# A fused top-k attention and two gated layers: the normalising half of the softmax one block later, two elementwise steps moved to ScalarE

## The chip, the cores and the metric

The kernel runs on one core of one Trainium2 chip. The metric is the device time of one execution in microseconds; the number of a kernel is the median of its runs. Engines are called as in the profile: PE (matmul) and PEld (its weight loads), DVE (VectorE), ACT (ScalarE), POOL (GpSimd), SP (which issues the DMAs here).

## What is computed

The reference is attention that keeps the 32 largest scores of each row, followed by two dense layers on the result. The shapes are 4 batches, 8 heads, 576 positions and a head size of 64; all 2304 rows of 512 values go through the layers.

```python
def _attn_ref(q, k, v):                      # top_k = 32, scale = 1 / sqrt(64)
    scores = scale * np.matmul(q, k.transpose(0, 1, 3, 2))
    kth = np.partition(scores, -top_k, axis=-1)[..., -top_k:-top_k + 1]
    scores = np.where(scores >= kth, scores, -1000000000.0)
    scores = scores - np.max(scores, axis=-1, keepdims=True)
    attn = np.exp(scores)
    attn = attn / (np.sum(attn, axis=-1, keepdims=True) + 1e-09)
    return np.matmul(attn, v)

def _moe_ref(x, w_gate, w_val, w_out):       # 512 -> 1536 -> 512
    gate = 1.0 / (1.0 + np.exp(-(x @ w_gate)))
    return gate * (x @ w_val) @ w_out

def _moe2_ref(x, w_in, w_out):               # 512 -> 2048 -> 512
    r = np.maximum(x @ w_in, 0.0)
    return (r * r) @ w_out
```

## The kernel before

**Tiling.** The 2304 rows are 18 tiles of 128 rows. `CHUNKS` groups them into 11 chunks: chunks 0 to 3 hold one tile each, chunks 4 to 10 two tiles. Attention works on a unit of one tile and one head, a "block" of 128 rows by 576 scores; there are 144 blocks, 8 in each of chunks 0 to 3 and 16 in each of chunks 4 to 10. Once all blocks of a chunk are through, the chunk goes through both layers (`moe`), while the blocks of the following chunks run beside it.

**One block.** `scores` (L313) multiplies queries and keys into one PSUM tile `sp` (a single buffer, L331), and ACT copies it to the SBUF tile `S` (two buffers, L334). `softmax` (L337) then finds the 32nd largest value on DVE: four MAX8 (L344), each giving the next eight maxima, with three MATCH_REPLACE8 (L350) between them, which strike out what was found. From the first and last maximum POOL makes the two biases `bs` (L354). ACT turns the scores below the threshold into a huge number (Relu, L357), POOL subtracts that from the scores (L358; this is the last reader of `S`), ACT takes the exponential and its row sum (L359). That is the first half. In the second half DVE adds 1e-9 to the sum (L363, tile `rz`) and inverts it (L366), and POOL multiplies the block with it, in two pieces (L375, `we` for the last 64 columns and `W` for the first 512). For chunks 4 and on (`DMT = 4`) ACT then rounds the block to fp16 (L381), POOL takes the remainder (L382), and a DMA on SP's queue transposes both (L387); for the second head of a pair the 64 end columns get the same treatment (L397 to L399), and the last unit of a pair issues the loads of the values (`load_values`). The matmul with the values is `values` (L471).

**Order of the blocks.** The generator `attention` (L965) issues, for block n: `head(n + 1)` (key and query loads, query transposes, scores and the copy to `S` of the next block), then `tail` of blocks that lag by two (`TLAG = 2`; at the end of a pair of heads its `values`), then `softmax` of block n. `last_max` holds the last MAX8 issued, and the first MAX8 of the next block is placed behind it, without a semaphore, so that DVE works on one block at a time.

**The layers.** In the first layer `l1_pair` (L686 on) makes two 128-wide columns of gate and value in PSUM (`pg`, `pv`, L705); ACT takes tanh (L715), POOL turns it into the scaled sigmoid by one addition and one multiplication (L716), DVE multiplies it with the value (L717), ACT rounds to fp16 (L720) and POOL takes the remainder (L721). In the second layer `l2_pair` (L803) PE makes `ph` (L812), ACT takes Relu (L821) and its square rounded to fp16 (L823), POOL squares Relu in fp32 in place (L824) and takes the remainder (L825). The products of `l1_acc` (L745) and `l2_acc` (L833) use both parts. Chunk 0 has a function of its own, `moe32`, which the diff leaves alone. Each chunk has 6 pairs in the first layer and 8 in the second; a pair is 128 by 512 in chunks 4 to 10 and 128 by 256 in chunks 1 to 3.

**What sets the order on the engines.** The program hands its instructions to a planner, which orders each engine's queue by the priority of the instruction (in the order of issue, attention moved ahead by `attend` with `AHEAD = 1000`) and by the time at which its own model of the chip has the operands ready. Each queue is then fixed and runs in order.

Of the kernel before, what the change touches and what calls it, by code (L numbers as in the profile page):

```python
# [10 lines left out]
F32 = mybir.dt.float32  # L11
# [3 lines left out]
AF = mybir.ActivationFunctionType  # L15
ALU = mybir.AluOpType
AX = mybir.AxisListType
PSUM = bass.MemoryType.PSUM
NOSYNC = mybir.DependencyInfo(mybir.DependencyClass.NoSync, mybir.DependencyReason.DATA)
DRAM = bass.MemoryType.DRAM  # L20

P = 128
# [42 lines left out]
DMT = 4  # L65
# [5 lines left out]
TB = 15  # L71
# [3 lines left out]
def tile_topk_attention__then__two_moe_layers(  # L75
# [14 lines left out]
    nc = tc.nc  # L90
# [20 lines left out]
    apool = ctx.enter_context(tc.tile_pool(name="apool", bufs=2))  # L111
# [134 lines left out]
    class Pair:  # L246
# [90 lines left out]
        def softmax(self, j, i, ss):  # L337
# [4 lines left out]
            cur = ss  # L342
            for r in range(TOPK // 8):
                m8 = nc.vector.max(mx[:, r], cur)  # L344
                if r == 0 and last_max:
                    tc.add_manual_dep(
                        m8.ins, last_max[0].name, NOSYNC, reason="one row block at a time"
                    )
                if r < TOPK // 8 - 1:
                    nc.vector.match_replace(wk, mx[:, r], cur, NEG)  # L350
                    cur = wk
            last_max[:] = [m8.ins]
            bs = apool.tile([P, 4], F32, tag="bs", bufs=3, name=f"bs_{tt}_{h}")
            nc.gpsimd.tensor_tensor(  # L354
                bs[:, 0:2], mx.rearrange("p a b -> p (a b)")[:, 0 : TOPK : TOPK - 1], bsc, op=ALU.mult
            )
# [2 lines left out]
            nc.scalar.activation(  # L359
                wk, wk, AF.Exp, bias=bs[:, 0:1], scale=SCALE, accum_out=bs[:, 2:3]  # L360
            )
            rz = apool.tile([P, 1], F32, tag="rz", bufs=3, name=f"rz_{tt}_{h}")
            nc.vector.tensor_scalar(  # L363
                rz, bs[:, 2:3], 1e-9, 1.0 if self.ci < DMT else 1.0 / PSC, op0=ALU.add, op1=ALU.mult
            )
            nc.vector.reciprocal(rz, rz)  # L366
            if self.ci < DIAG:
                dg = apool.tile([P, P], F32, tag="we", bufs=WE, name=f"dg_{tt}_{h}")
                nc.gpsimd.tensor_scalar(dg, ident, rz, 1.0, op0=ALU.mult, op1=ALU.mult)
                return wk, dg  # L370
# [315 lines left out]
    def moe_head(ci, x):  # L686
        m = ahead[ci] = Moe()
        m.gp, m.queue = None, []
        tts = chunks[ci]
        N = len(tts) * P  # L690
        ig = scales["wg"][1]
        xs, ix = x
        gsc = mpool.tile([P, 1], F32, tag="gsc", bufs=2, name=f"gsc_{ci}")
        nc.vector.scalar_tensor_tensor(gsc, ix, 0.5, ig, op0=ALU.mult, op1=ALU.mult)

        def l1_pair(fp, gh=None):
            pg = ps_w.tile([P, 512], F32, tag="wk", name=f"pg_{ci}_{fp}")
            pv = ps_w.tile([P, 512], F32, tag="wk", name=f"pv_{ci}_{fp}")
            for pp, wd in ((pg, "wg"), (pv, "wv")):
                for e in range(2):  # L700
                    f0 = (2 * fp + e) * P
                    n = 0
                    for c in range(KM):
                        for a, b_ in SPLIT:
                            nc.tensor.matmul(  # L705
                                pp[:, e * N : (e + 1) * N],
                                wblk(wd, a, c, f0, P),
                                xs[:, b_, c, :],
                                start=(e == 0 and n == 0),
                                stop=(n == 3 * KM - 1),  # L710
                                skip_group_check=True,
                            )
                            n += 1
            th = mpool.tile([P, 2 * N], F32, tag="f32w", bufs=2, name=f"th_{ci}_{fp}")
            nc.scalar.activation(th, pg[:, 0 : 2 * N], AF.Tanh, scale=gsc)  # L715
            nc.gpsimd.tensor_scalar(th, th, 1.0, float(2.0 ** (-TB - 1)), op0=ALU.add, op1=ALU.mult)  # L716
            nc.vector.tensor_tensor(th, pv[:, 0 : 2 * N], th, op=ALU.mult)  # L717
            if gh is None:
                gh = mpool.tile([P, 2, 2 * N], F16, tag="hi", bufs=HIB, name=f"gh_{ci}_{fp}")
            nc.scalar.copy(gh[:, 0], th)  # L720
            nc.gpsimd.tensor_tensor(gh[:, 1], th, gh[:, 0], op=ALU.subtract)  # L721
            return gh

        m.N, m.ix, m.l1_pair = N, ix, l1_pair

    def moe(ci, nxt=None):
# [76 lines left out]
        def l2_pair(fp):  # L803
# [17 lines left out]
            nc.scalar.activation(r, ph[:, 0 : 2 * N], AF.Relu, scale=float(2.0 ** (7 - 2 * TB)))  # L821
            gh = mpool.tile([P, 2, 2 * N], F16, tag="hi", bufs=HIB, name=f"rh_{ci}_{fp}")
            nc.scalar.activation(gh[:, 0], r, AF.Square)  # L823
            nc.gpsimd.tensor_tensor(r, r, r, op=ALU.mult)  # L824
            nc.gpsimd.tensor_tensor(gh[:, 1], r, gh[:, 0], op=ALU.subtract)  # L825
            return gh

# [137 lines left out]
    def attention():  # L965
# [10 lines left out]
        ready = {}  # L976
        work = {}
        lagging = []

        def keys(pi):  # L980
            if pi < len(pairs):
# [63 lines left out]
        for n, (pr, pi, j, i) in enumerate(units):  # L1045
            with tc.high_priority(offset=int(up[0])):
                head(n + 1)
                while lagging and n - lagging[0] >= (TLAG if units[lagging[0]][0].ci >= DMT else 1):
                    tail(lagging.pop(0))
            work[n] = pr.softmax(j, i, ready.pop(n))  # L1050
            lagging.append(n)
            yield
        while lagging:
            tail(lagging.pop(0))
        yield
# [145 lines left out]
```

## Time and profile before

| | us |
|---|---|
| three runs | 1345.93, 1340.33, 1340.26 |
| their median | 1340.33 |
| the profiled execution, its own time | 1336.54 |
| the span of its trace | 1334.4 |
| busy: PE, DVE, POOL, ACT | 1180.9, 1045.8, 953.4, 791.8 |
| mean granted clock of TensorE, share of full speed | 0.938 |

The trace covers the span; 2.1 us of the profiled execution lie outside it. A share of busy time is a mean over stages with different limits: the first 300 us also prepare the weights, up to 1165 us attention and layers run side by side, and after that only the layers of the last two chunks are left. A wait is put down to the instruction that released it.

### The profile page before, as it was taken

What the parts mean: (1) busy time and instruction counts of PE and PEld (TensorE: products, weight loads), DVE (VectorE), ACT (ScalarE), POOL (GpSimd) and SP (SyncE); (2) the same over time, 40 slices, a digit from 0 to 9 for tenths busy, and PEclk for the clock granted to TensorE, in tenths of its full rate; (3) what the DMA queues carried; (4) which work ended last, traced back from release to release, by engine and by line L of the source; (5) the groups of instructions that cost most, each with busy time, mean ns of one, the idle gap of its engine ahead of it and who ended that gap; (6) DMA issues with size and microseconds to landing.
All of it is one profiled execution on the core that took longest, in us unless ns stands there. A gap on an engine that the chain in (4) does not pass through costs nothing. (4 is left out here: it accounts for less than half of the span.)

```text
span 1334.4 us, 28839 instructions
## 1 busy us (share of the span) xinstructions
PE 1180.9 (88%) x10525; PEld 939.5 (70%) x10525; DVE 1045.8 (78%) x2258; ACT 791.8 (59%) x1592; POOL 953.4 (71%) x1164
## 2 busy tenths in 40 slices
PE   6657878978979889899965999999999999999998
PEld 4535766767868858667853767776876787787775
DVE  6999999999898988978889887888898988601010
ACT  4875767777666666655645665665666666523122
POOL 1887877886678797778767795787879788824223
PEclk9755989989999999999985999999999999999999
DMA  6967871256566765596854667787465655330300
GB/s 187 347 248 246 269 208 43 76 185 229 175 194 148 172 167 108 123 219 155 200 111 109 150 157 162 152 209 159 101 165 128 115 126 141 74 126 1 142 1 16
DMA packets 260717, 201.66 MB, mean 151 GB/s; under 512 B 205536, under 2 KB 213728, under 8 KB 260576
## 3 DMA queue, kind: packets, MB, share of 16 engines
q1 hardware_dynamic: 260576, 199.82, 56.1%
q8 instruction: 83, 1.36, 0.4%
q14 instruction: 58, 0.48, 0.1%
HBM read 143.65 MB, written 23.07 MB: 125 GB/s over the span
## 5 line engine op out<-in xcount | busy, mean ns | idle before, releaser
L344 DVE MAX8 mx<-W 128x8 f32<-128x576 f32 x432 | 327.3, 758 | 8.2
L358 POOL TENSOR_TENSOR W<-S,W 128x576 f32<-128x576 f32 x144 | 206.9, 1437 | 42.2 <-ACT W L357 35.7
L812 PE MATMUL ph<-x,wi_w 128*128 128x256 f16 (+1 forms) x1920 | 206.7, 261 | 9.4 <-ACT x L784 7.3
L350 DVE MATCH_REPLACE8 W<-mx,W 128x576 f32<-128x576 f32 x288 | 213.7, 742 | 0.0
L833 PE MATMUL acc<-w2t,rh 128*128 128x512 f16 x816 | 196.4, 382 | 5.9 <-DMA w2t<-w2s 5.4
L812 PEld LDWEIGHTS <-wi_w 128*128 128x128 f16 x1920 | 168.1, 100 | 42.0 <-issue 11.6
L331 PE MATMUL sp<-kst,qt 128*128 128x288 f32 x608 | 130.0, 334 | 32.2 <-ACT S L334 27.9
L705 PE MATMUL pg<-xs,wg_w 128*128 128x256 f16 (+1 forms) x1440 | 156.4, 260 | 2.1 <-POOL xs L669 1.1
L705 PE MATMUL pv<-xs,wv_w 128*128 128x256 f16 (+1 forms) x1440 | 152.5, 257 | 1.6 <-ACT th L715 0.6
L359 ACT ACTIVATE W<-W,bs 128x576 f32<-128x576 f32 x144 | 111.5, 775 | 67.8 <-POOL W L358 67.2
L357 ACT ACTIVATE W<-S,bs 128x576 f32<-128x576 f32 x144 | 111.4, 774 | 56.2 <-POOL bs L354 55.6
L382 POOL TENSOR_TENSOR w<-W,w 128x512 f16<-128x512 f32 x112 | 131.0, 1170 | 17.1 <-ACT w L381 16.8
L745 PEld LDWEIGHTS <-wo_w 128*128 128x128 f16 x1440 | 124.6, 99 | 25.1 <-issue 12.0
L705 PEld LDWEIGHTS <-wg_w 128*128 128x128 f16 x1440 | 124.5, 99 | 20.5 <-issue 2.2
L705 PEld LDWEIGHTS <-wv_w 128*128 128x128 f16 x1440 | 122.8, 98 | 20.4 <-issue 5.7
L833 PEld LDWEIGHTS <-rh 128*128 128x128 f16 x816 | 77.9, 98 | 83.5 <-issue 4.1
L745 PE MATMUL acc<-gh,wo_w 128*128 128x256 f16 (+1 forms) x1200 | 123.5, 257 | 10.1 <-POOL gh L721 8.2
L331 PEld LDWEIGHTS sp<-kst,qt 128*128 128x128 f32 x608 | 93.3, 200 | 44.6 <-ACT S L334 31.0
L344 DVE MAX8 mx<-S 128x8 f32<-128x576 f32 x144 | 107.4, 746 | 13.6 <-ACT S L334 13.5
L824 POOL TENSOR_TENSOR r<-r 128x512 f32<-128x512 f32 (+1 forms) x80 | 73.4, 919 | 57.4 <-ACT rh L823 57.2
L717 DVE TENSOR_TENSOR th<-pv,th 128x512 f32<-128x512 f32 (+1 forms) x60 | 36.2, 603 | 98.7 <-PE pv L705 96.0
L350 DVE MATCH_REPLACE8 W<-mx,S 128x576 f32<-128x576 f32 x144 | 106.9, 743 | 0.3 <-issue 0.3
(325 smaller groups left out, 2202.9 us busy)
## 6 DMA issues: line engine op xcount, KB each, us to landing
w2t<-w2s SPq DMA_DIRECT2D x80, 512.0 KB, 5.0
kst<-ks SPq DMA_DIRECT2D x104, 288.0 KB, 3.1
v<-vs SPq DMA_DIRECT2D x40, 288.0 KB, 3.3
qn<-in_q_dram SPq DMA_DIRECT2D x128, 64.0 KB, 2.6
wi_r<-in_moe_w_in_dram SPq DMA_DIRECT2D x16, 512.0 KB, 6.9
w_r<-in_moe_w_out_dram SPq DMA_DIRECT2D x16, 512.0 KB, 4.4
wg_r<-in_moe_w_gate_dram SPq DMA_DIRECT2D x12, 512.0 KB, 7.8
wv_r<-in_moe_w_val_dram SPq DMA_DIRECT2D x12, 512.0 KB, 6.7
```

The costliest lines, as they stand in the source:

```text
L331: nc.tensor.matmul(sp[:, e, 0:HALF], l, r, start=(x == 0), stop=(x == len(ops) - 1))
L344: m8 = nc.vector.max(mx[:, r], cur)
L350: nc.vector.match_replace(wk, mx[:, r], cur, NEG)
L357: nc.scalar.activation(wk, ss, AF.Relu, bias=bs[:, 1:2], scale=-BIG)
L358: nc.gpsimd.tensor_tensor(wk, ss, wk, op=ALU.subtract)
L359: nc.scalar.activation(wk, wk, AF.Exp, bias=bs[:, 0:1], scale=SCALE, accum_out=bs[:, 2:3])
L382: nc.gpsimd.tensor_tensor(w16[:, 1], wk[:, 0:SM], w16[:, 0], op=ALU.subtract)
L705: nc.tensor.matmul(pp[:, e * N : (e + 1) * N], wblk(wd, a, c, f0, P), xs[:, b_, c, :], start=(e == 0 and n == 0), stop=(n == 3 * KM - 1), ...
L745: nc.tensor.matmul(acc[:, d // 2, (d % 2) * N : (d % 2 + 1) * N], wblk("wo", a, f, d * P, P), gh[:, b_, e * N : (e + 1) * N], start=(f == ...
L812: nc.tensor.matmul(ph[:, e * N : (e + 1) * N], wblk("wi", a, c, f0, P), x2[:, b_, c, :], start=(e == 0 and n == 0), stop=(n == 3 * KM - 1) ...
L824: nc.gpsimd.tensor_tensor(r, r, r, op=ALU.mult)
L833: nc.tensor.matmul(acc2[:, i, 0:DM], gh[:, b_, e * N + i * P : e * N + (i + 1) * P], w2t[fp][:, a, e, :], start=(f == 0 and x == 0), stop= ...
```

## The change

The second half of `softmax` becomes a method `weigh`. For chunks 4 and on it is issued after the first half of the next block: in the order of issue it moves behind `head` of the block after next, behind the `tail` calls there, and behind the four MAX8, three MATCH_REPLACE8, the biases, Relu, subtraction and exponential of the next block. Its addition (L363 before) is placed, without a semaphore, behind the second MAX8 of the next block. The biases get a fourth buffer. In the first layer the scaling of tanh goes from POOL to ACT (`Copy` with scale and bias), in the second the square in fp32 goes from POOL to ACT (`Square`).

```diff
@@ softmax
                 m8 = nc.vector.max(mx[:, r], cur)
+                if r == 1:
+                    second = m8.ins
...
-            last_max[:] = [m8.ins]
-            bs = apool.tile([P, 4], F32, tag="bs", bufs=3, name=f"bs_{tt}_{h}")
+            last_max[:] = [m8.ins, second]
+            bs = apool.tile([P, 4], F32, tag="bs", bufs=4, name=f"bs_{tt}_{h}")
...
+            if self.ci >= DMT:
+                return wk, bs
+            return self.weigh(j, i, wk, bs)
+
+        def weigh(self, j, i, wk, bs):
+            tt = self.tts[i]
+            h = 2 * self.hp + j
             rz = apool.tile([P, 1], F32, tag="rz", bufs=3, name=f"rz_{tt}_{h}")
-            nc.vector.tensor_scalar(
+            add = nc.vector.tensor_scalar(
                 rz, bs[:, 2:3], 1e-9, 1.0 if self.ci < DMT else 1.0 / PSC, op0=ALU.add, op1=ALU.mult
             )
             nc.vector.reciprocal(rz, rz)
+            if self.ci >= DMT and last_max[1:]:
+                tc.add_manual_dep(
+                    add.ins, last_max[1].name, NOSYNC, reason="not before the next row block's start"
+                )
@@ l1_pair
-            nc.gpsimd.tensor_scalar(th, th, 1.0, float(2.0 ** (-TB - 1)), op0=ALU.add, op1=ALU.mult)
+            k = float(2.0 ** (-TB - 1))
+            nc.scalar.activation(th, th, AF.Copy, scale=k, bias=k)
@@ l2_pair
-            nc.gpsimd.tensor_tensor(r, r, r, op=ALU.mult)
+            nc.scalar.activation(r, r, AF.Square)
@@ attention
+        late = []
...
             work[n] = pr.softmax(j, i, ready.pop(n))
+            if late:
+                m = late.pop()
+                work[m] = units[m][0].weigh(*units[m][2:], *work[m])
+            if pr.ci >= DMT:
+                late.append(n)
             lagging.append(n)
             yield
+        for m in late:
+            work[m] = units[m][0].weigh(*units[m][2:], *work[m])
```

## Rows read from the trace of the kernel before

**Rows 1.** Busy time by stretch: stretch and length, engines, granted clock, DMA share, GB/s.

```profile
360.00:700.00 340.00, 303.95 (x3165) 245.59 (x3164) 299.17 (x692) 210.76 (x452) 259.99 (x364) 0.96 0.67 160
700.00:730.00 30.00, 13.30 (x92) 9.73 (x93) 27.55 (x68) 18.40 (x38) 20.84 (x30) 0.50 0.47 112
730.00:1283.00 553.00, 539.52 (x4574) 423.92 (x4574) 380.19 (x853) 299.27 (x583) 388.56 (x494) 0.99 0.52 128
```

**Rows 2.** Timeline of PE, 690 to 711 us: start, length, instruction, wait before it.

```profile
691.07 0.80 PE L331 MATMUL sp<-kst,qt 128*128 128x288 f32 x4 [2.00 <-ACT S L334]
...
710.54 1.33 PE L331 MATMUL sp<-kst,qt 128*128 128x288 f32 x4 [7.30 <-ACT S L334]
```

**Rows 3.** Line 363 from 360 to 700 us: its instructions, what DVE waited for.

```profile
L363 DVE TENSOR_SCALAR rz<-bs x48: 128/145/155, 363.2 to 698.5; 128x1 f32<-128x1 f32 x48
...
  ACT W L359: 15.1, 14
```

**Rows 4.** Timeline, 594 to 600 us: one of the 14 waits, ACT and POOL before.

```profile
594.49 1.15 POOL L382 TENSOR_TENSOR w<-W,w 128x512 f16<-128x512 f32 x1
...
595.61 1.40 POOL L358 TENSOR_TENSOR W<-S,W 128x576 f32<-128x576 f32 x1
...
597.49 0.60 ACT L821 ACTIVATE r<-ph 128x512 f32<-128x512 f32 x1 [3.11 <-PE ph L812]
597.98 0.77 ACT L359 ACTIVATE W<-W,bs 128x576 f32<-128x576 f32 x1
...
598.74 0.63 ACT L334 COPY S<-sp 128x576 f32<-128x576 f32 x1
598.87 0.15 DVE L363 TENSOR_SCALAR rz<-bs 128x1 f32<-128x1 f32 x1 [2.16 <-ACT W L359]
...
599.40 0.76 DVE L344 MAX8 mx<-S 128x8 f32<-128x576 f32 x1 [0.18 <-ACT S L334]
```

**Rows 5.** Timeline around the first and the last of those 14 waits.

```profile
400.97 0.61 ACT L334 COPY S<-sp 128x576 f32<-128x576 f32 x1
...
401.09 0.15 DVE L363 TENSOR_SCALAR rz<-bs 128x1 f32<-128x1 f32 x1 [1.24 <-ACT W L359]
...
401.89 0.74 DVE L344 MAX8 mx<-S 128x8 f32<-128x576 f32 x1
...
690.38 0.64 ACT L334 COPY S<-sp 128x576 f32<-128x576 f32 x1
690.52 0.15 DVE L363 TENSOR_SCALAR rz<-bs 128x1 f32<-128x1 f32 x1 [1.58 <-ACT W L359]
...
692.12 0.74 DVE L344 MAX8 mx<-S 128x8 f32<-128x576 f32 x1
```

**Rows 6.** Groups by line and shape, whole span: POOL's two steps that the change moves.

```profile
L824 POOL TENSOR_TENSOR r<-r 128x512 f32<-128x512 f32 x56 | 58.2, 1040 | 53.8 <-ACT rh L823 53.7
...
L716 POOL TENSOR_SCALAR th<-th 128x512 f32<-128x512 f32 x42 | 25.9, 617 | 43.2 <-ACT th L715 39.7 <-ACT vnb L206 2.0 <-DMA kst<-ks 1.2
```

**Rows 7.** Groups by line and shape, whole span: the nearest work that ACT does already.

```profile
L381 ACT CAST w<-W 128x512 f16<-128x512 f32 x112 | 69.1, 617 | 26.3 <-POOL W L375 22.2 <-DMA PT<-w 3.6
L823 ACT ACTIVATE rh<-r 128x512 f16<-128x512 f32 x56 | 35.3, 630 | 1.8 <-PE acc L833 0.7
...
L823 ACT ACTIVATE rh<-r 128x256 f16<-128x256 f32 x24 | 10.0, 416 | 2.5 <-PE acc L833 2.1
```

**Rows 8.** Lines 716 and 824 from 360 to 700 us: how many of each shape.

```profile
L716 POOL TENSOR_SCALAR th<-th x20: 398/613/622, 365.9 to 676.7; 128x512 f32<-128x512 f32 x12, 128x256 f32<-128x256 f32 x8
...
L824 POOL TENSOR_TENSOR r<-r x24: 606/618/1045, 390.7 to 615.1; 128x256 f32<-128x256 f32 x16, 128x512 f32<-128x512 f32 x8
```

**Rows 9.** Timeline of POOL at 468 us: a moved step ahead of a block's subtraction.

```profile
468.51 0.61 POOL L824 TENSOR_TENSOR r<-r 128x256 f32<-128x256 f32 x1
469.08 1.41 POOL L358 TENSOR_TENSOR W<-S,W 128x576 f32<-128x576 f32 x1
```

**Rows 10.** Waits, whole span: PE for the transposed weights; total, times, longest.

```profile
PE xp L471 <- DMA PT<-w: 10.5, 8, 2.4
```

## The prediction

> **What bounds the kernel now.** I read the busy time by stretch first. After 730 us PE is the bound: it is busy for 539.5 of 553 us at a granted clock of 0.99 [rows 1], so nothing that DVE, POOL or ACT win there can come back as more than the 13.5 us that PE is idle. From 360 to 700 us nothing is that full: PE is busy for 304.0 of 340 us and DVE for 299.2. Which of the two leads is shown by what lies at the end of this stretch, and for that I read PE's timeline. Between 690 and 711 us four matmuls of `scores` wait 2.0, 4.7, 4.0 and 7.3 us, 18.0 together, for ACT's copy to `S` [rows 2], where the first and the last of the four stand. PE has used up the layers of chunk 5, and chunk 6 has not come out of attention. While PE waits, DVE works for 27.6 of the 30 us from 700 on, POOL for 20.8 and ACT for 18.4 [rows 1]. So up to about 710 us the end is set by the loop that carries the softmax: DVE's seven passes over a block and the chain by which DVE gets its next `S`. What that loop gains there comes off the end nearly one for one, and behind it 604 us of PE work follow that the change doesn't touch. The reader should see two regimes: before 710 us the softmax loop, after it PE.
>
> Next I read what DVE waits for in the first regime. Of its waits the largest is at the addition that opens the second half of the softmax: 48 such additions from 360 to 700 us, and 14 of them make DVE stand still for 15.1 us in all, each for the exponential on ACT [rows 3]. That is the wait which the first part of the change could remove.
>
> **Part one, the second half one block later.** The 15.1 us are not what can be won. ACT works in order, and the copy to the `S` that DVE's next block needs stands right behind the exponential: the exponential frees nothing, but its subtraction on POOL was the last reader of the old `S`, and both become ready together. At 598.87 us DVE's addition begins after 2.16 us of waiting, the copy ends at 598.74 + 0.63 = 599.37 us, and the next block's first MAX8 begins at 599.40 us [rows 4]. Take the addition away and that MAX8 still begins at 599.40: the gain is nothing. So I went through all 14 on the timeline, taking for each the smaller of the wait itself and the time from the end of that copy (and 0.07 us for the signal) to the next MAX8. The first: 401.89 - (400.97 + 0.61 + 0.07) = 0.24 of its 1.24 us; the last: 692.12 - (690.38 + 0.64 + 0.07) = 1.03 of its 1.58 us [rows 5]. Over the 14 the sum is 5.4 us; ten of them give under 0.35 us each. Bounds: 0, if the addition keeps its place in the queue, and 15.1. I take 5.4, because it is worked out wait by wait.
>
> The addition does not move far. Counted over the 112 blocks of chunks 4 to 10 on DVE's timeline, it already stands behind the third MAX8 of the next block 59 times, behind the fourth 37 times, behind the second 13 times and before the second only 3 times. The new order (not before the second MAX8) is thus met 109 times in 112. What changes is the priority: the addition, the inversion, POOL's two multiplications and its remainder, ACT's rounding, the end columns, SP's transposing DMAs and value loads now come after the next block's biases, Relu, subtraction and exponential, and on SP's queue after the key and query loads and the layer-two weight loads that `head` and the layers put there. That helps where POOL does the remainder of the old block just ahead of the subtraction of the new one: L382 for 1.15 us, then L358 [rows 4]. It is worth between 0 and 1.15 us in each of a few blocks, and where POOL would not have been ready anyway it is worth nothing; I take 1.0 us, ends 0 and 3. Its price would be later transposes; that is a rival below.
>
> **Part two, two steps from POOL to ACT.** A 128 by 512 square costs POOL 1.040 us and the scaling of tanh 0.617 us [rows 6]. The trace has no ACT Copy with a bias and no in-place fp32 square; nearest are the rounding L381 with 0.617 us and the rounding square L823 with 0.630 us, and 0.416 us for the half-width shape [rows 7]. I use these. From 360 to 700 us there are 20 scalings, 12 of them wide, and 24 squares, 8 of them wide [rows 8]. ACT gains 12 x 0.617 + 8 x 0.416 + 8 x 0.630 + 16 x 0.416 = 22.4 us and goes from 210.8 to 233 us of 340, still under DVE. POOL, at 260.0 us, loses these 44 steps.
>
> What POOL's relief is worth: a moved step stands directly ahead of the subtraction of a block that ends in one of the 14 waits, as at 468.51 us, where a square of 0.61 us holds L358 up to 469.08 [rows 9]. This is so in three places (the waits at 420, 471 and 488 us), 0.6 us each, less what was counted above: 1.7 us. In the other long waits (479, 510, 599 and 690 us) ACT itself stood still in its queue, for a DMA or for PE, as for 3.11 us before L821 [rows 4]; no lighter POOL cures that. Ends 0 and 5.
>
> What ACT's load costs: I put each new piece behind its L715 or L823 and carried the delay along until ACT's next idle time had eaten it. Of 49 copies to `S` from 360 to 700 us only three (at 401, 420 and 616 us) are then later than their MAX8 can bear, by 0.7 us in all. I take 0.7; ends 0 and 22.4. The cover is ACT's idle time, 340 - 210.8 = 129 us [rows 1]; if it is gone, the cost is the upper end.
>
> The Trainium skill speaks against this part: "TensorE: Matmul & The Clock Gate", in the section on the array's architectural detail, says that ScalarE's queue is strictly first in, first out. The trace agrees (the ready exponential at 597.98 us stands behind L821). By that rule alone each piece would push everything behind it, and the sum would have +22.4 us in place of +0.7.
>
> **The sum.** Waits at the addition -5.4, priority -1.0, POOL's relief -1.7, ACT's load +0.7: -7.4 us. PE's clock adds to it: from 700 to 730 us PE works 13.3 us at a granted 0.50, its lower level of 1.2 GHz, after the waits just told [rows 1]; at 2.4 GHz these would be 6.65 us. If the 18.0 us of waits shrink by 7.4, a part of 6.65 us goes too: at most 6.65, in proportion 2.7; I take 2. In all -9.4 us. The profiled execution took 1336.54 us, of which 1334.4 are the span, and would take 1327.1; it lies 3.8 us under the median of the three runs, and carried over to that median of 1340.33 the forecast is 1330.9, say 1331 us.
>
> **The rivals.** *The next wait takes it all.* The copy behind the exponential holds DVE in every one of the 14 places, or the planner leaves the addition where it is (109 of 112 already obey the new order): 0 to -4 us, 1336 to 1340 us. For it: ten of 14 waits give next to nothing. Against it: the 1.0 us that the last of them gives lies right in PE's long wait.
>
> *Transposed weights come late (slower).* PE waits 8 times, 10.5 us in all, for `PT` [rows 10], and after 730 us it is the bound. If the second half sinks behind the next block's fourth MAX8 (a replace and a MAX8 more, 1.6 us) and behind its subtraction on POOL (1.40 us [rows 4]), each of these waits grows by 3.0 us: 24 us, less 9.4, gives +14.6, so 1355 us. It turns the sign past 0.5% once the delay is over (9.4 + 6.7) / 8 = 2.0 us. For it: the second half has lost its priority on four queues. Against it: between a block's second half and its `values` lie two blocks before and still one after.
>
> *ACT's queue (slower).* In order, all 22.4 us of new work reach the loop: 1340.3 - 8.1 - 2 + 22.4 = 1353 us. For it: ACT carries every copy from PSUM. Against it: 129 us of idle time, and only 3 of 49 copies without slack.
>
> *The hand-over clears up.* A new plan may bring chunk 6 out in time; then the 18.0 us of waits and 6.65 us of slow clock go: 1340.3 - 24.7 = 1315.6 us.
>
> **How the numbers follow.** A measurement of this kernel can tell about 0.5% (6.7 us) from no change, so the bound of faster is 1333.6 us. Partial gain, as forecast: 0.46, of which 0.34 lies under that bound and 0.12 above. Hand-over cleared: 0.10. Next wait takes it: 0.20. Late weights 0.16, ACT's queue 0.08. So faster 0.34 + 0.10 = 0.44, same 0.12 + 0.20 = 0.32, slower 0.24. The range goes from 1310, a little under the cleared hand-over, to 1355, which takes in both slower cases at their price and leaves out what is worse; the forecast's own range is 1324 to 1338.
>
> **What would show it.** Right: the waits at the addition fall from 15.1 us to under 4, while DVE's waits for the copy to `S` grow by most of that; PE's waits from 690 to 711 us fall by about 7 us and no more; POOL's busy time falls by at least the 84 us of the wide shapes [rows 6], and ACT's rises by at least 61 (42 x 0.617 + 56 x 0.630). Wrong: DVE still waits for the exponential at the addition (the planner left it there); PE's waits for `PT` rise well above 10.5 us; or PE is idle for over 20 us after 730 us, for then its queue and not the softmax loop would set the end.

## The result, and the profile after

The changed kernel takes 1317.53 us (median of three: 1314.45, 1317.53, 1324.27) where the kernel before takes 1340.33: a ratio of 0.983, 95% interval 0.980 to 0.987, or 22.8 us less. The forecast was 1331 us. The direction was right, the size was not: 9.4 us were forecast.

One caution on the pair of traces. The profiled execution of the changed kernel is the slowest of its three (1324.27 us, span 1322.5), and that of before, 1336.54 us, lies 3.8 us under its median. The pair shows 11.9 of the 22.8 us. Where a few us matter I therefore read two more profiles: `again`, the changed kernel once more (span 1315.7), and `bs4`, which orders every engine's queue exactly as the kernel before does (span 1336.8).

Busy time of the changed kernel by stretch, columns as in [rows 1]:

```profile
360.00:700.00 340.00, 305.50 (x3166) 246.64 (x3163) 304.15 (x708) 234.62 (x508) 237.38 (x329) 0.96 0.68 159
700.00:730.00 30.00, 19.64 (x146) 14.85 (x146) 27.44 (x66) 20.29 (x43) 20.86 (x28) 0.63 0.61 143
730.00:1283.00 553.00, 541.48 (x4581) 425.06 (x4580) 374.33 (x848) 334.51 (x648) 327.30 (x419) 0.99 0.50 125
```

Against [rows 1], PE is busy for 19.6 in place of 13.3 us from 700 to 730, at a granted 0.63 in place of 0.50, and for 2 us more behind 730. POOL has 22.6 us less to do from 360 to 700 us and ACT 23.9 us more, as the counts of [rows 8] said (22.4).

PE around the hand-over of chunk 6 (timeline: start, length, instruction, wait before it), which answers to [rows 2]:

```profile
691.94 1.33 PE L331 MATMUL sp<-kst,qt 128*128 128x288 f32 x4 [1.73 <-ACT S L334]
...
696.94 1.33 PE L331 MATMUL sp<-kst,qt 128*128 128x288 f32 x4 [3.67 <-ACT S L334]
...
702.25 1.44 PE L484 MATMUL xp<-PT,v 128*64 128x128 f16 x23 [3.99 <-DMA PT<-w]
```

Two waits for the copy to `S` are left, 5.4 of 18.0 us; a wait of 4.0 us for the transposed weights has come. The values of the last pair of chunk 6 now stand behind one set of later scores in PE's queue, where they stood behind four.

The addition, now line 372, in the stretch of [rows 3], and PE's two waits over the whole span, the first of which answers to [rows 10] (total, times, longest):

```profile
L372 DVE TENSOR_SCALAR rz<-bs x49: 134/144/154, 364.2 to 696.5; 128x1 f32<-128x1 f32 x49
...
  ACT W L361: 9.0, 10
```

```profile
PE xp L484 <- DMA PT<-w: 18.6, 16, 4.0
...
PE sp L331 <- ACT S L334: 16.8, 11, 3.8
```

The kernel before had this for the copy:

```profile
PE sp L331 <- ACT S L334: 30.6, 13, 7.3
```

So DVE still waits 9.0 us at the addition, PE waits 8.1 us more for the weights, and 13.8 us less for the copy to `S`.

Chunk 6 does leave DVE earlier. Its last MAX8 in the kernel before, in the changed kernel and in `again` (timeline of DVE):

```profile
697.12 0.76 DVE L344 MAX8 mx<-W 128x8 f32<-128x576 f32 x1
...
691.97 0.76 DVE L344 MAX8 mx<-W 128x8 f32<-128x576 f32 x1
...
688.61 0.76 DVE L344 MAX8 mx<-W 128x8 f32<-128x576 f32 x1
```

It ends 5.2 and 8.5 us earlier, and PE gets through more work at the hand-over. The stretch from 690 to 735 us in `bs4` and in `again`, then what is left for PE behind it in `again`:

```profile
690.00:735.00 45.00, 19.17 (x127) 14.38 (x128) 40.74 (x97) 25.32 (x52) 29.88 (x42) 0.58 0.43 101
...
690.00:735.00 45.00, 28.78 (x233) 22.63 (x234) 41.88 (x102) 29.80 (x60) 32.39 (x43) 0.68 0.56 129
735.00:1400.00 665.00, 566.99 (x4724) 439.55 (x4721) 366.32 (x829) 341.64 (x658) 329.38 (x418) 1.00 0.42 103
```

In `bs4` PE has 4839 instructions and 579.3 us of work left at 735 us (its row stands under "Where part one wins"), in `again` 4724 and 567.0, in the changed kernel's first trace 4762 and 571.6. So up to 12.3 of the 21.1 us by which the trace of `again` is shorter than that of `bs4`, and up to 7.8 of the 14.3 us of the first trace, are there at 735 us.

The two moved steps cost on ACT (groups by line and shape: count, busy us, mean ns, idle before them):

```profile
L838 ACT ACTIVATE r<-r 128x512 f32<-128x512 f32 x56 | 35.2, 629 | 1.0
...
L730 ACT ACTIVATE th<-th 128x512 f32<-128x512 f32 x42 | 26.5, 631 | 0.8
```

That is the price the forecast took from the nearest rows [rows 7]. The page gives POOL 850.3 us of busy time (953.4 before) and ACT 857.1 (791.8).

### The profile page after: what moved, and what is told of

Read it like the earlier page. It is cut to its first block, busy times and chain, and to the rows that moved or that the text cites. A ratio compares the mean times of both kernels' runs of the same rounds, so it can differ in the third digit from the quotient of the medians.

```text
span 1322.5 us, 28809 instructions
## 1 busy us (share of the span) xinstructions
PE 1180.5 (89%) x10525; PEld 937.6 (71%) x10525; DVE 1039.8 (79%) x2258; ACT 857.1 (65%) x1732; POOL 850.3 (64%) x1024
## 4 chain that ended last, share of the span: by engine, by line
PE 48%; DVE 13%; DMA 7%; POOL 7%; ACT 6%; issue 3%; SPq 2%; ACTq 0%; DVEq 0%; POOLq 0%
PE acc L847 10%; PE ph L826 9%; PE pg L718 7%; PE pv L718 6%; PE acc L759 6%; DVE mx L344 5%; DVE W L352 4%; DMA PT<-w 4%; PE xp L484 4%; PE sp L331 3%; POOL W L360 2%; DMA vn<-in_v_dram 2%; POOL w L395 1%; DMA w2t<-w2s 1%; POOL W L388 1%
## 5 line engine op out<-in xcount | busy, mean ns | idle before, releaser
L839 POOL TENSOR_TENSOR rh<-r,rh 128x512 f16<-128x512 f32 (+1 forms) x80 | 81.1, 1014 | 74.9 <-ACT r L838 68.6
```

## The experiments

The theories, with the letters that some of the expectations use. **A**: the forecast, DVE loses its waits at the addition up to 710 us and the end follows. **B**: POOL's lighter load does it. **C**: any edit makes the planner order everything anew, and the new order happens to be better. **D**: what counts is that the next block's loads, scores and copy to `S` go first on the queues. **E**: what counts is where the values stand among later blocks' scores in PE's queue. Ratios are to the kernel before, with 95% intervals. "Part one" is the later second half, "part two" the two steps on ACT.

**The parts alone, and the change again.** `again` is the changed kernel. `part1` leaves the two steps on POOL:

```diff
-            k = float(2.0 ** (-TB - 1))
-            nc.scalar.activation(th, th, AF.Copy, scale=k, bias=k)
+            nc.gpsimd.tensor_scalar(th, th, 1.0, float(2.0 ** (-TB - 1)), op0=ALU.add, op1=ALU.mult)
...
-            nc.scalar.activation(r, r, AF.Square)
+            nc.gpsimd.tensor_tensor(r, r, r, op=ALU.mult)
```

`part2` is the kernel before with the opposite of this diff and nothing else. `nodep` is the changed kernel without the placement behind the second MAX8:

```diff
-            if self.ci >= DMT and last_max[1:]:
-                tc.add_manual_dep(
-                    add.ins, last_max[1].name, NOSYNC, reason="not before the next row block's start"
-                )
```

`again`, expected:

> The changed kernel once more, beside the others on one chip, because its three times lay 10 us apart (1314 to 1324) and its profiled execution was the slowest of them: span 12 us under the one before, median 23 us under. If the median tells the truth, five rounds give a ratio of 0.981 to 0.986; if the profiled pair does, 0.989 to 0.992.

`part1`, expected:

> Only the second half of the softmax one block later; tanh's scaling and the fp32 square stay on POOL. Theory A (the forecast's own terms: waits at the addition 5.4 us, priority 1, clock 2, all from this part): 6 to 9 us faster, ratio 0.993 to 0.996. Theory B (what counts is POOL's load, 70% of the span, in the chain between a block's last maximum and its exponential): ratio 0.998 to 1.003, since POOL does the same work. Theory C (the new plan of all queues has its own luck, up to 10 us either way): anything, and the two parts don't add up to the whole.

`part2`, expected:

> Only the two steps from POOL to ACT; the softmax stays whole. Theory A: POOL's relief 1.7 us less ACT's load 0.7 us, so ratio 0.998 to 1.000. Theory B: most of the gain, ratio 0.984 to 0.990, with POOL's subtraction (a block's last maximum to the end of its exponential) visibly shorter. Theory C: no relation to part one; the product of the two ratios differs from that of the whole by over 0.5%.

`nodep`, expected:

> The changed kernel without the placement behind the second maximum. Before, 109 of 112 additions stood behind it anyway. Theory A: within 0.3% of the changed kernel (ratio 0.981 to 0.988 to the one before). If the placement is what keeps DVE from standing still, the waits at the addition grow back towards 15 us from 360 to 700 us and the ratio is 0.99 or more.

Measured: `again` 0.983 (0.980 to 0.985), `part1` 0.984 (0.982 to 0.987), `part2` 0.9977 (0.9962 to 0.9993), `nodep` 0.982 (0.980 to 0.985). The parts multiply to 0.982, the whole. Part one is the change, part two gives 3 us, and the placement nothing. B falls as the main cause, and so does the rival that ACT's queue pays for part two. What DVE waits for from 360 to 700 us in `part1` (total, times, longest):

```profile
DVE qt L307 <- ACT qt L306: 9.9, 7, 2.8
DVE rz L372 <- ACT W L361: 7.5, 7, 1.9
DVE mx L344 <- ACT S L334: 4.5, 6, 2.1
DVE vs_0n L135 <- ACT vnq L208: 4.2, 2, 3.6
```

The wait at the addition has halved (15.1 before), but the copies of the query transposes hold DVE for 9.9 us (7.4 before) and those of a value step for 4.2 (none before). DVE is busy for 296.6 us of this stretch, so idle for 43.4, and was idle for 340 - 299.2 = 40.8; the last MAX8 of chunk 6 ends at 700.6 us and ended at 697.9. Part one alone wins 1.6%, over twice what A expected of it, without DVE being a single microsecond earlier at the point where the forecast looked for the gain. In `part2` that MAX8 ends at 701.4 us; of these kernels only those with both parts bring chunk 6 out earlier. As the account of part one, A is in doubt.

**Buffers, and half of the move.** `bs4` is the kernel before with only the fourth bias buffer; `s3` is it with a third buffer for `S`, which takes away what the copy waits for; `after_s3` is the changed kernel with the same. `mid` is `part1` without the placement and issues the second half just ahead of the next block's first half, so that it moves only past `head` and the `tail` calls:

```diff
+            if late:
+                m = late.pop()
+                work[m] = units[m][0].weigh(*units[m][2:], *work[m])
             work[n] = pr.softmax(j, i, ready.pop(n))
-            if late:
-                m = late.pop()
-                work[m] = units[m][0].weigh(*units[m][2:], *work[m])
```

`bs4`, expected:

> The kernel before with only the fourth buffer for the biases. The order of the instructions on every engine is that of the kernel before, so it is a control and a second trace of it: ratio 0.997 to 1.003. The profiled execution of the kernel before (1336.5 us) lay under all but none of 17 later ones (1338 to 1348); this one should lie within that band, and show where the missing 5 to 10 us sit: by theory A in PE's waits and slow clock at 690 to 735 us.

`s3`, expected:

> The kernel before with three S buffers: the copy of the next scores no longer waits for the subtraction of a block and need not stand behind its exponential. The forecast said that this copy makes 10 of 15 us of waits at the addition worthless. Theory A: DVE's waits for the copy to S and PE's waits for it at 690 to 711 us shrink, 5 to 12 us faster, ratio 0.991 to 0.996. If DVE's waits before 710 us are not what sets the end: 0.998 to 1.002.

`after_s3`, expected:

> The changed kernel with three S buffers. Theory A: the copy behind the exponential is what holds DVE now that the addition waits less, so a further 5 to 10 us: ratio 0.974 to 0.979 to the kernel before. If the gain of part one already came from freeing the copy (theory D), nothing more: 0.981 to 0.985.

`mid`, expected:

> Part one with the second half issued just ahead of the first half of the next block, not behind it (and no placement behind the second maximum): it is moved past the head of the block after next (key and query loads, scores, the copy to S) and the tail, and no more. If what counts is that the next block's biases, Relu, subtraction and exponential come first (theory A), this gives at most 2 us: ratio 0.997 to 1.002. If what counts is that the next scores and their copy come first (theory D: the head), it gives what part one gives: 0.982 to 0.988.

Measured: `bs4` 0.998 (0.9967 to 1.0001), no change, as it should be with the same order on every queue. `s3` 0.994 (0.992 to 0.996), `after_s3` 0.988 (0.985 to 0.991), `mid` 0.994 (0.992 to 0.996). A third `S` buffer, which cuts PE's waits for the copy from 30.6 to 15.9 us in `s3`, helps the kernel before by 0.6% and costs the changed one 0.6%: PE's waits for the copy are not the price of the old order by themselves. `s3` lies in the range that A asked for, but not by A's way: the last MAX8 of chunk 6 ends at 702.6 us there, later than before. `after_s3` lies above both of its ranges. `mid` lies between its two: by this run, going past the next block's loads and scores is worth about a third of part one, and the rest comes from going past its first half. D would be a third of the answer, unless any new plan wins as much (see "What stays open").

**The place of the values.** `b_end` and `b_all` are the kernel before with `tail` issued ahead of `head` and the next set of scores placed behind the values by a dependence without a semaphore, for the last pair of each chunk or for all pairs (chunks 4 to 10). `a_sw2` is the changed kernel with `tail` issued ahead of `head`; `a_end4` lets the values of each chunk's last pair lag by four blocks in place of two:

```diff
+                    if e == 0 and x == 0 and last_val:
+                        tc.add_manual_dep(
+                            mm.ins, last_val.pop().name, NOSYNC, reason="not ahead of a chunk's last values"
+                        )
...
+            if self.ci >= DMT:
+                last_val[:] = [vmm.ins]
```

```diff
+            return 4 if pr.hp == NHP - 1 and j == 1 and i == len(pr.tts) - 1 else TLAG
```

`b_end`, expected:

> The kernel before, with one thing of its order changed: on PE's queue the values of a chunk's last pair may not stand behind the scores of more than two later blocks. Before, chunk 6's last values stand behind four sets of scores (80 to 83), in every kernel with part one behind one. Theory E (part one wins by where the values stand between the scores on PE's in-order queue): the 21 us that PE waits for the copy to S from 680 to 735 us fall under 10, and a third to two thirds of part one's gain appears without part one: ratio 0.987 to 0.995. Theory A (DVE's waits at the addition, POOL's order): 0.998 to 1.003.

`b_all`, expected:

> The same for the values of every pair from chunk 4 on, so that no values stand behind more than two sets of later scores (before: up to four, 1.9 in the mean; here 1.1). Theory E: as the former and a little more, 0.984 to 0.993, unless PE now waits for the transposed weights instead: more than 20 us of such waits (10 before) would eat it, 0.995 to 1.003. Theory A: 0.998 to 1.003.

`a_sw2`, expected:

> An attempt at a faster version: the changed kernel with the tail (the values) issued ahead of the next head, so that the values stand behind 1.36 sets of later scores in the mean (changed kernel 1.46, before 1.89). Theory E: the same or up to 4 us faster than the changed kernel, ratio 0.979 to 0.984; if PE's waits for the transposed weights grow by more than the others shrink, 0.984 to 0.988.

`a_end4`, expected:

> The changed kernel, with the values of a chunk's last pair issued two blocks later, so that on PE's queue they stand behind 6, 4, 5, 5, 2, 2 sets of later scores (chunks 4 to 9) in place of 2, 1, 1, 2, 2, 2. Nothing else is undone: DVE, POOL and ACT keep the second half one block later. Theory E: most of the gain goes, 10 to 25 us slower than the changed kernel, ratio 0.990 to 1.001 to the kernel before. Theory A: at most 5 us slower, ratio 0.982 to 0.987.

Measured: `b_end` 1.009 (1.006 to 1.011), `b_all` 1.059 (1.056 to 1.062), `a_sw2` 0.994 (0.992 to 0.996), `a_end4` 0.992 (0.990 to 0.995). Every placement is worse than the one the planner made in the kernel that it starts from, early or late. PE's waits behind 360 us in `b_all` show why early is bad:

```profile
PE xp L476 <- DMA PT<-w: 31.5, 16, 6.2
PE sp L332 <- ACT S L339: 18.2, 11, 6.3
PE acc L840 <- DMA w2t<-w2s: 16.0, 7, 8.2
PE x2pq L785 <- ACT x L783: 15.9, 5, 9.1
PE vpq L207 <- ACT vnb L206: 12.1, 2, 10.4
```

PE takes its queue in order: values that stand early wait for their weights, and the scores and the layers behind them wait too. Values that stand late cost as well: `a_end4` gives some 12 us back, as E expected and A did not. But E expected a gain of `b_end` and `b_all`, and they lose. E, the place alone, falls as the whole cause; that the place counts is borne out.

**Where part one wins.** `hi` is `part1` with the later second half for chunks 7 to 10 only, which run after about 700 us; `lo` is the other half, chunks 4 to 6. `wB` is `part1` with the addition, the inversion and POOL's two multiplications left in the first half, so that only the rounding, the remainder, the end columns, the DMAs and the value loads go later.

```diff
-            if self.ci >= DMT:
+            if self.ci >= 7:
                 return wk, bs
...
-            if pr.ci >= DMT:
+            if pr.ci >= 7:
                 late.append(n)
```

`lo`, expected:

> Part one alone, and only for the blocks of chunks 4 to 6, which run before about 700 us; chunks 7 to 10 keep the second half in its old place. Two regimes, as the forecast has them (the softmax loop sets the end up to about 710 us, and after that PE has nothing to give): all of part one's gain is here, ratio 0.982 to 0.987. Late regime (part one wins by the work behind 735 us, where PE's idle time fell from 17.9 to 8.6 us): less than half of the gain is here, 0.991 to 0.996, and the rest in the run with chunks 7 to 10. Hand-over: PE's waits for the copy to S between 690 and 712 us fall from 18 to under 10 us, since chunk 6's last values stand behind one set of later scores in place of four.

`hi`, expected:

> Part one alone, and only for the blocks of chunks 7 to 10, which run after about 700 us. Two regimes: nothing, 0.998 to 1.002; chunk 6's last values stay behind four sets of later scores, as in the kernel before. Late regime: 0.990 to 0.994, and PE's idle time behind 735 us falls from 17.9 to under 11 us.

`wB`, expected:

> Part one alone with the addition, the inversion and POOL's two multiplications left in the first half; only the rounding, the remainder, the end columns, the transposing DMAs and the loads of the values go one block later. If part one wins because DVE's queue is freed of the addition (the forecast's mechanism): 0.996 to 1.001, since the addition is where it was. If it wins because the rounding, the remainder and the DMAs give way to the next block's first half, and the values take another place among the scores on PE: 0.983 to 0.989, as part one whole; DVE's waits at the addition stay above 12 us all the same.

Measured: `lo` 0.998 (0.997 to 0.9999), `hi` 0.987 (0.985 to 0.989), `wB` 0.995 (0.993 to 0.997). Used only up to 700 us, part one is worth about 2 us; used only after it, 17. This is the reverse of what the forecast said, and goes beyond the ranges of the late regime too. First `lo`: the addition from 360 to 700 us, then PE's two waits over the whole span.

```profile
L372 DVE TENSOR_SCALAR rz<-bs x48: 129/143/154, 365.4 to 699.5; 128x1 f32<-128x1 f32 x48
...
  ACT W L361: 6.6, 7
```

```profile
PE xp L484 <- DMA PT<-w: 26.7, 13, 7.8
...
PE sp L331 <- ACT S L334: 16.0, 14, 4.0
```

DVE's waits at the addition fall from 15.1 to 6.6 us and PE's waits for the copy from 30.6 to 16.0, and little comes of it: the waits for the weights rise from 10.5 to 26.7. At the hand-over of chunk 6 two waits for the copy are left, 4.5 us (below 10, as expected), and behind them come 5.4 us for a value step (`vnb`) and 3.7 for the weights. From its first MAX8 of chunk 4 to its last of chunk 6 DVE takes 335.3 us, and took 336.4. In this stretch the forecast's first rival is what happens in `lo`, the next wait takes nearly all of it.

Then the stretch behind 735 us, to the end: first its busy time in `bs4`, then in `hi`.

```profile
735.00:1400.00 665.00, 579.30 (x4839) 449.74 (x4836) 378.98 (x853) 310.76 (x602) 402.47 (x504) 0.99 0.43 107
```

```profile
735.00:1400.00 665.00, 574.46 (x4832) 448.02 (x4830) 378.13 (x850) 308.05 (x593) 401.87 (x504) 1.00 0.43 105
```

`bs4` ends at 1336.8, `hi` at 1321.4 us. From 735 on PE is therefore idle for 1336.8 - 735 - 579.3 = 22.5 us in `bs4` and for 11.9 in `hi`, and busy for 4.8 us less. That the two make up the 15.4 us between the spans is arithmetic. What shows that the gain arises behind 735 us is that `hi` changes nothing ahead of chunk 7 and that PE has as many instructions left at 735, 4832 and 4839. More than half of it is there by 939 us: from 700 us on PE is then busy for 219.1 us (1901 instructions) in `hi` and for 210.7 (1757) in `bs4`. Where the 4.8 us of busy time come from isn't shown; the granted clock of the stretch is 0.99 in `bs4` and 1.00 in `hi`. (The waits alone fall from 17.6 to 6.8 us.) PE's longest waits in this stretch, `bs4` and then `hi`:

```profile
PE xp L471 <- DMA PT<-w: 5.8, 3, 3.0
PE x2pq L778 <- ACT x L776: 3.2, 4, 1.2
PE ph L812 <- ACT x L784: 2.1, 2, 1.6
PE sp L331 <- DMA kst<-ks: 1.8, 1, 1.8
PE kpt L169 <- DMA kn<-in_k_dram: 1.7, 1, 1.7
PE pg L705 <- POOL xs L669: 0.8, 1, 0.8
```

```profile
PE x2pq L791 <- ACT x L789: 2.2, 4, 0.7
PE ph L825 <- ACT x L797: 1.6, 1, 1.6
PE sp L331 <- ACT W L359: 1.3, 1, 1.3
PE xp L484 <- DMA PT<-w: 0.9, 1, 0.9
```

No wait is large; part one takes away a handful of 1 to 3 us each. The waits for the weights fall here although their second half is issued later, and those for the key loads (`kn`, `kst`) go: these loads now stand ahead of the moved DMAs in the order of issue, which would explain it; no run tests that. DVE is freer too: from the first MAX8 of block 80 to that of block 112 (chunks 7 and 8) it takes 221.8 us in place of 240.3, and its idle time there falls by 18.3 us, of which 8 are at the addition (11.1 to 3.1 us).

`wB` gets 6 of part one's 21 us, between its two expectations, with the addition where it was and DVE waiting for 13.5 us there from 360 to 700. By this run the rounding, the remainder and the DMAs do a third of it, and it matters that the addition, the inversion and POOL's multiplications go later too.

**What DVE's time is worth.** If the softmax loop set the end, DVE work added to it would come out at the end. `d1`, `d2` and `d3` are the kernel before with one more MAX8 per block in chunks 5 and 6, 7 and 8, 9 and 10; its result is not used.

```diff
+            if self.ci in (5, 6):
+                m8 = nc.vector.max(apool.tile([P, 8], F32, tag="mxe", bufs=2, name=f"mxe_{tt}_{h}"), ss)
             last_max[:] = [m8.ins]
```

`d1`, expected:

> The kernel before with one more MAX8 over S in each of the 32 blocks of chunks 5 and 6 (about 465 to 698 us), its result not used: 32 times 0.75 = 24 us more of DVE, behind the fourth MAX8. By the forecast's two regimes the softmax loop sets the end here: most of the 24 us come out at the end, ratio 1.012 to 1.018. The same by the reading that the softmax loop sets the end from 360 to 930 us.

`d2`, expected:

> The same 24 us of DVE in the 32 blocks of chunks 7 and 8 (about 698 to 936 us). By the forecast's two regimes PE sets the end here and DVE's 20 to 34 us of idle time take it: 1.000 to 1.004. By the reading that the softmax loop still sets the end here (part one made these 32 blocks 18 to 20 us shorter and 11 to 12 us of that reached the end): 1.008 to 1.018.

`d3`, expected:

> The same 24 us of DVE in the 32 blocks of chunks 9 and 10 (about 936 to 1150 us), where part one made the blocks no shorter and PE is idle for 4 us. By both readings PE sets the end here: 0.999 to 1.005. If it is 1.008 or more, the softmax loop sets the end up to 1150 us.

Measured: `d1` 1.003 (1.002 to 1.004), `d2` 0.999 (0.998 to 1.001), `d3` 1.0005 (0.998 to 1.003). 24 us more on DVE cost 4 us in the first stretch, far less than the 1.012 that the forecast's regimes asked for, and nothing in the other two. The loop itself takes up a part of them: in `d1` the last MAX8 of chunk 6 ends at 709.9 us, 11.5 us later than in `bs4`. Busy time from 700 to 939 us, `bs4` and then `d2`:

```profile
700.00:939.00 239.00, 210.67 (x1757) 160.94 (x1758) 201.12 (x461) 146.32 (x301) 182.32 (x241) 0.93 0.68 157
```

```profile
700.00:939.00 239.00, 210.70 (x1715) 159.91 (x1715) 211.86 (x485) 145.50 (x297) 179.73 (x237) 0.91 0.63 152
```

DVE works 10.7 us more in this stretch. PE is busy for as long as before but begins 42 instructions fewer; they come later, and behind 735 us it is idle for 15.0 us in `d2` in place of 22.5. Of the 24 us, the blocks of chunks 7 and 8 get longer by 6, DVE's idle time takes 8, and the rest is work of the layers on DVE that slides behind. DVE's work is not the bound in any of the three stretches. What the time of the loop is worth is less clear: `d1` made it 11.5 us longer and the end came 4 us later, `d2` 6 us longer and the end came no later, and each of these kernels also has a plan of its own.

**What stays open.** The gain of part one is PE time behind 735 us (`hi`). It is not DVE's work (`d2`). Nor is it the place of chunk 6's values, which `hi` leaves behind four sets of scores; but those of chunk 7's first two pairs, behind four and three sets in `bs4`, stand behind one and two in `hi`, so that the place of later values isn't ruled out as a part of it. Beside that, what remains is that the moved steps give way to the next block's first half and loads on four queues, and that the planner, given the new order, lays out chunks 7 to 10 differently on PE. These two come together in every kernel that I ran. Some of that PE time can be had with no second half moved: `s3` keeps the issue order of before, and with one more buffer and a new plan PE's waits behind 735 us fall from 17.6 (`bs4`) to 9.9 us, for a gain of 0.6%; `s3`, `mid` and `wB`, three unlike edits, all win 0.5 to 0.6%. So C may hold for a part of the 17 us, though more than that came each time in `part1`, `hi` and `again`, whose orders on PE differ. To tell them apart one would have to run the new issue order with the old queue on PE, which wasn't tried. For the whole change a second point is open: in its traces about half of the gain is there at 735 us, while `lo` and `part2`, each by itself, win only 2 and 3 us at the end. What the earlier hand-over is worth there would be shown by `lo` with part two, which wasn't run.

## Why the prediction was wrong, step by step

**The direction and part two were right.** Part two was put at -1.0 us (-1.7 for POOL, +0.7 for ACT); `part2` measures 0.9977, some 3 us with 2 us of uncertainty. The durations taken from the nearest rows held (617 and 630 ns forecast, 631 and 629 measured). The signs named for it came: POOL's busy time fell by 103 us (at least 84 were asked), ACT's rose by 65 (at least 61).

**ACT's queue** was the rival that went by the Trainium skill's sentence, in "TensorE: Matmul & The Clock Gate" (the section on the array's architectural detail), that ScalarE's queue is strictly first in, first out. By that rule alone 22.4 us would have come on top. ACT did get 23.9 us more work from 360 to 700 us and the kernel did not get slower. The forecast's own reckoning fits that: in order, but with 105 us of idle time left in the stretch, a piece moves what stands behind it and the next idle time eats the delay. The delays themselves were not traced.

**A step that part one alone does not bear out: 5.4 us at the addition, and "what that loop gains there comes off the end nearly one for one."** It rested on PE's 18.0 us of waits at the hand-over [rows 2] and on DVE being busy for 27.6 of the 30 us after 700 [rows 1]. With part one alone the 5.4 us, worked out wait by wait, hardly reach the loop. In `lo` the waits at the addition fall by 8.5 us, but DVE gets through chunks 4 to 6 only 1.1 us faster, and the end moves by 2 us; in `part1` DVE is 1.7 us slower there. In `lo` PE's waits for the copy fall by 14.6 us and its waits for the weights rise by 16.2: I had costed that rival at its wait on DVE's side (the copy behind the exponential), and it came on PE's as well. With both parts the loop does get shorter, by 4.2 us from chunk 4 to chunk 6 in the changed kernel's first trace and by 6.9 in `again` (7.4 were forecast), and PE is up to 7.8 and 12.3 us of work ahead at 735 us. So the mechanism of the forecast does show in the whole change, at about its size; what each of the two parts does for it, and how much of it reaches the end, isn't shown. `d1` gives the rate the other way round, 4 us at the end for 11.5 us at the end of the loop, under a plan of its own.

**The step that failed: PE's waits after 730 us, entered as nothing.** "Nothing [...] can come back as more than the 13.5 us that PE is idle" was used as a reason to put zero, when it was an upper bound of the size of the whole gain; to the end of the span the idle time was 1334.4 - 730 - 539.5 - 44.3 = 20.6 us, since the stretch of [rows 1] stopped at 1283 us and PE was busy for 44.3 us behind it; the "604 us of PE work" hold these 20.6. `hi`, which leaves everything ahead of chunk 7 as it was, shows 10.6 us of idle time and 4.8 us of busy time won there, and 17 us between the medians. This alone is more than the 13.4 us by which the forecast fell short. A busy share of 0.976 on an engine that works in order says that it is the bound; it doesn't say that the rest can't be had. Half of that bound would have been 10 us more, and a forecast of 1321 us.

**The clock** was put at -2 us. By the forecast's reckoning PE lost 13.3 x 0.50 = 6.65 us to it from 700 to 730 us before and loses 19.64 x (1 - 0.63) = 7.3 us after: the granted clock of the stretch is higher and PE's waits in it are shorter, but more work falls into it. So reckoned, the term is no gain.

**The signs that were named.** Waits at the addition "under 4 us": 9.0, and the copy's waits on DVE did not take the rest (4.3 to 3.4 us from 360 to 700 us). PE's waits at 690 to 711 us "by about 7": those for the copy fell by 12.6, of which 4.4 came back as waits for the weights. "`PT` well above 10.5": 18.6, so the rival of late weights did come true as a mechanism, at 8 of its 24 us, and was outweighed; its price was set by a delay on DVE and POOL, while `hi`, with all of that delay in chunks 7 to 10, has only 3.8 us of it in all. "PE is idle for over 20 us after 730 us" was a sign that the kernel before gave already, with 20.6; after the change it is 1322.5 - 730 - 576.6 = 15.9. The cleared hand-over, the only rival on this side, gave 1315.6 us, near the result, and its mechanism came in part: `again` has 106 more of PE's instructions between 690 and 735 us than `bs4`. But `part1` has 4817 left at 735, 22 fewer than `bs4`, and ends within 3 us of the changed kernel, so that the rival's number came close by luck as far as these runs show. `lo` doesn't settle it, since its own hand-over isn't cleared: the waits told above are 13.6 us there, against 18.0.

Two readings in the forecast were a little off. The 0.07 us for the signal stand in no row: in the trace DVE's MAX8 begins 0.03 us behind the copy that it waited for in 20 of 24 cases and 0.10 in the others, and with 0.03 the 5.4 us would be 5.6. And 107 of the 112 additions stand behind the second MAX8 of the next block, where 109 were counted; as `nodep` shows, nothing hangs on it.

## What to carry to other kernels

Where an engine works in order and is 97% busy, price its last 3% wait by wait, to the end of the span, before calling a stage closed: here several waits of 1 to 3 us, each for another producer, went together in one change of the order. And before a wait on another engine is put into the sum, ask for the rate at which that engine's time reaches the end; a kernel with some work added to it measures that rate, if one also reads how much later the engine's own loop ends. Leave the planner its order unless a run shows a better one: the four orders that I made by hand were all worse than the one they started from.

## What the runs showed of the hardware

An fp32 `Copy` with scale and bias and an fp32 `Square` in place cost ACT 631 and 629 ns for 128 by 512, and the rounding square 628; POOL took 617 and 1040 ns for the same two steps [rows 6]. The square is the better one to move. Executions of one and the same kernel differ: the three of the changed kernel have spans of 1322.5, 1312.6 and 1315.7 us at mean granted clocks of 0.941, 0.947 and 0.944. There the shorter span has the higher clock, but in `nodep` the shortest of five (1312.3 us) has the lowest, 0.938, and the longest (1320.5 us) has 0.946. So a pair of single traces can't settle a difference of a few us, and the mean clock alone doesn't explain it.
